# Hash attention and mixer: the products with v in four column tiles of 32, and one score block that begins with the bits

## The chip, the core and the metric

The kernel runs on one NeuronCore of a Trainium2 chip. The metric is the device time of one execution in microseconds; several executions are taken and the median is given. A profile of one execution comes with it: its span goes from the first to the last instruction of the program, and its engines are PE (TensorE, matrix products; PEld is its weight-load stream), DVE (VectorE), ACT (ScalarE), POOL (GpSimd) and SP (SyncE, which here only issues transfers).

## The reference

Attention over 4 batches, 8 heads, 768 tokens and 64 channels a head, in which a query sees only the keys of its own hash bucket, and then one mixer block whose input is the attention's output.

```python
q_bits = (einsum('bhsd,dk->bhsk', q, proj) > 0)      # 6 bits a token; k_bits likewise
mask   = q_bucket[..., :, None] == k_bucket[..., None, :]
scores = where(mask, q @ k.T / sqrt(64), -1e9)
attn   = softmax(scores)
x      = (attn @ v), heads side by side: (4, 768, 512)
h      = relu(x.T @ w_tok1) @ w_tok2                 # mixes tokens
u      = x + h.T
out    = u + relu(u @ w_ch1) @ w_ch2                 # mixes channels
```

All inputs but the four weight matrices are float32; the weights arrive as 64-bit floats and are turned into float32 on the chip.

## The kernel before

The program has three stages, one after the other: attention (from about 4 to 315 us of the span), the token mixing (to about 393 us) and the channel mixing. The change lies in attention alone.

Attention works on 16 pairs of heads (`pairs`, 4 batches by 4 pairs of heads). In a pair, q and k of both heads lie transposed in one tile, head i in partitions 64i to 64i+63. The 768 queries are cut into two halves of 384 (`Half`), the 768 keys into six blocks of 128 (`NR`). The order of the work is that of the program text: the stage runs under a manual schedule, and each engine works through its own instructions in the order in which the loop at L461 writes them.

For each half, `scores` (L328) makes six blocks. A block is a tile `sc` of 128 keys by two heads by 384 queries in PSUM, from a ring of three. Two products are added up in it: `product` at L334 with q and k (float32, 64 rows by 128 columns, one product a head, the two heads side by side in the array), and the same with `bits` (bf16). The rows of `bits` hold plus or minus one half for the query and a large multiple of it for the key, with one more row that cancels the sum when all bits agree, so that a key in another bucket gets a score so low that its exponential is zero. `exponential` (L342) takes the block to `e` on ACT, a tile in a ring of twelve. `add` and `add_last` sum the six tiles `e` of a half on DVE.

`hashes` (L292) makes the bits for the next pair: four products of 32 columns side by side (`hp`), a comparison on DVE (`g`), a scaling on ACT, and eight small transfers on SP into the rows of `bits` (L308). Block 0 of the next pair reads rows that the first four of these fill, the blocks from 3 on also those of the last four.

`weigh` (L380) multiplies with v: for each of six key blocks and each head one float32 product with the 64 columns of v as the weights, head 0 into partitions 0 to 63 of `acc` and head 1 into 64 to 127, so two column tiles of 64 side by side. ACT then takes `acc` to `num`. `Quotients.sums` (L407) sums the exponentials over keys with four products of 32 columns, `newton` and `divide` turn them into reciprocals and the result.

PE's order in pairs 1 to 14 is: six blocks of half 0, six blocks of half 1, `sums` of the pair before, `hashes` of the pair after, `weigh` of half 0, `weigh` of half 1. Pair 0 has no `sums` and makes its own hashes early; in its first half the first three blocks wait for those (`first`). Pair 15 makes no hashes and runs `sums`, `weigh`, `sums`, `weigh`. A float32 product appears in the trace as two matmul records and two weight loads, a bf16 product as one of each.

Of the kernel before, what the change touches and what calls it, by code (L numbers as in the profile page):

```python
# [48 lines left out]
def kernel(  # L49
# [13 lines left out]
    nc = tc.nc  # L63
    P = 128
    B, NP, _, _, S = qk.shape
    D = 64
# [4 lines left out]
    NR = S // P  # L71
# [186 lines left out]
    def attention(pool, psum, W1, W2, x0):  # L258
# [53 lines left out]
        def first_hashes(which, half):  # L312

            sl = slice(HALF * half, HALF * half + HALF)
            ps = psum.tile([P, 512], F32, name="hw", tag="sm" if which else "acc", bufs=1)[:, :HALF]
            nc.tensor.matmul(ps, projwide, loaded[0][0][:, which, sl], start=True, stop=True)  # L316
            to = bitrows[0][:, which, sl]
            nc.vector.tensor_scalar(to, ps, 0.0, 0.5, op0=ALU.is_gt, op1=ALU.subtract)  # L318
            if which:
                nc.vector.tensor_scalar(to, to, widescale, None, op0=ALU.mult)  # L320

        class Half:
# [5 lines left out]
            def scores(self):  # L328

                qkt, bits = loaded[self.n][0], bitrows[self.n % 2]  # L330
                qs = slice(HALF * self.half, HALF * self.half + HALF)
                first = self.n == self.half == 0

                def product(sc, t, c, start):  # L334
                    for i in range(2):
                        rows = slice(D * i, D * i + D)
                        nc.tensor.matmul(  # L337
                            sc[:, i, :HALF], t[rows, 1, P * c : P * c + P], t[rows, 0, qs],
                            start=start, stop=not start,
                        )  # L340

                def exponential(sc):  # L342
                    e = pool.tile([P, 2, HALF], F32, name="e", tag="e", bufs=12)
                    nc.scalar.activation(e, sc[:, :, :HALF], ACT.Exp, scale=SCALE)  # L344
                    self.es.append(e)

                waiting = []
                if first:
                    first_hashes(0, 0)
                    first_hashes(1, 0)  # L350
                for c in range(NR):
                    sc = psum.tile([P, 2, 512], F32, name="sc", tag="sc", bufs=3)
                    product(sc, qkt, c, True)
                    if first and c < GR:
                        waiting.append((c, sc))
                        if c == GR - 1:
                            for c, sc in waiting:
                                product(sc, bits, c, False)
                                exponential(sc)
                            first_hashes(1, 1)  # L360
                        continue
                    product(sc, bits, c, False)
                    exponential(sc)
                if first:
                    first_hashes(0, 1)
# [14 lines left out]
            def weigh(self):  # L380

                _, vn, _, vsum = loaded[self.n]
                if self.half:
                    acc = psum.tile([P, 2, 512], F32, name="acc", tag="sc", bufs=3)[:, 0, :HALF]
                else:
                    acc = psum.tile([P, 512], F32, name="acc", tag="acc", bufs=1)[:, :HALF]
                for c, e in enumerate(self.es):
                    for i in range(2):
                        nc.tensor.matmul(  # L389
                            acc[D * i : D * i + D], vn[:, i, c], e[:, i],  # L390
                            start=(c == 0), stop=(c == NR - 1),
                        )
                if self.half == 0:
                    nums[self.n] = pool.tile([P, 2, HALF], F32, name="num", tag="num", bufs=2)
                nc.scalar.activation(  # L395
                    nums[self.n][:, self.half], acc, ACT.Identity, scale=-1.0, bias=vsum,
                )
# [1057 lines left out]
```

## Time and profile before

| | |
|---|---|
| median of the runs | 802.52 us (3 runs, 801.86 to 803.08) |
| span of the profiled execution | 801.2 us |
| PE busy | 792.6 us, 99% of the span, 3885 matmuls |
| products with v (L389) | 768 matmul records of 488 ns, 768 weight loads of 137 ns |
| q-k products (L337) | 768 matmul records of 487 ns |
| bits' products (L337) | 384 matmul records of 323 ns |
| DVE busy, ACT busy | 657.8 us (82%), 441.6 us (55%) |
| exponentials (L344) | 192 of 811 ns |
| granted TensorE clock | 0.997 of full speed |

The profiled execution's own time was not recorded apart from its span; the median of the runs is 1.3 us above the span. A matmul's recorded length contains the time[...]the next one already runs, so the pace of PE is read from the starts of its records, not from their lengths. "64*128" beside a matmul is the rows by columns of the array that it uses. In brackets stands how long the engine was idle before and what released it.

### The profile page before, as it was taken

Reading aid. Unit: us, or ns where it says so; the run is one execution under the profiler, and the core shown is the slowest. Engines: PE = TensorE matmul, PEld = TensorE weight load, DVE = VectorE, ACT = ScalarE, POOL = GpSimd, SP = SyncE. Lnnn points to the kernel's source line nnn. Section 1 sums busy time; section 2 is a strip of 40 time slices with the busy share of each in tenths; the row PEclk is TensorE's granted clock in tenths of the full one; section 3 lists DMA queues with packets and bytes.
Section 4 is the critical chain, followed back from the end, with each engine's and each line's share of the span. In section 5 each row is a group of like instructions: output and inputs, shape, how many; then the busy total and the mean of one; then the engine's idle time right before and its main releaser. Section 6 shows DMA issues by size and latency. Waiting matters only on the chain.

```text
span 801.2 us, 10593 instructions
## 1 busy us (share of the span) xinstructions
PE 792.6 (99%) x3885; PEld 470.7 (59%) x3885; DVE 657.8 (82%) x881; ACT 441.6 (55%) x707; POOL 53.7 (7%) x77
## 2 busy tenths in 40 slices
PE   9999999999999999999999999999999999999996
PEld 5444444444444444455544458876667886666885
DVE  4889898989887677999677888988769897779986
ACT  5688888888888887333222221327783335775111
POOL 1000000000000000011121010011110012000010
PEclk9999999999999999999999999999999999999998
DMA  4435353537352424797636994599754578630455
GB/s 163 159 122 160 121 161 121 161 121 239 125 169 87 149 73 161 199 290 180 155 69 207 305 377 173 175 302 273 222 143 145 216 202 192 216 106 9 164 177 132
DMA packets 90972, 138.61 MB, mean 173 GB/s; under 512 B 29656, under 2 KB 63392, under 8 KB 88608
## 3 DMA queue, kind: packets, MB, share of 16 engines
q1 hardware_dynamic: 82480, 112.47, 42.4%
q0 software_dynamic: 7728, 24.64, 13.9%
q10 hardware_dynamic: 704, 0.74, 0.3%
q8 instruction: 33, 0.54, 0.3%
q14 instruction: 27, 0.22, 0.1%
HBM read 97.21 MB, written 33.16 MB: 163 GB/s over the span
## 4 chain that ended last, share of the span: by engine, by line
PE 99%; DVE 0%; ACT 0%; issue 0%
PE b L761 50%; PE sc L337 20%; PE acc L389 16%; PE t L634 5%; PE t L674 5%; PE sums L413 2%; PE hp L298 1%; PE hw L316 0%; PE idle L451 0%; DVE second L1184 0%; DVE bits L318 0%; ACT second L679 0%; DVE bits L320 0%; DVE ones L97 0%; PE b L1300 0%
## 5 line engine op out<-in xcount | busy, mean ns | idle before, releaser
L344 ACT ACTIVATE e<-sc 128x768 f32<-128x768 f32 x192 | 154.0, 811 | 12.4 <-PE sc L337 12.1
L337 PE MATMUL sc<-qk 64*128 64x384 f32 x768 | 156.7, 487 | 0.0
L761 PE MATMUL b<-R,second 128*128 128x256 f32 (+1 forms) x612 | 150.9, 404 | 0.0
L761 PEld LDWEIGHTS b<-R,second 128*128 128x128 f32 x612 | 116.3, 190 | 31.6 <-issue 17.2
L767 ACT COPY c<-b 128x512 f32<-128x512 f32 (+1 forms) x78 | 37.4, 488 | 169.1 <-PE b L761 158.5
L389 PE MATMUL acc<-e,vn 128*64 128x384 f32 x768 | 127.6, 488 | 0.0
L375 DVE TENSOR_TENSOR esd<-esd,e 128x768 f32<-128x768 f32 x96 | 92.0, 958 | 10.0
L389 PEld LDWEIGHTS acc<-e,vn 128*64 128x64 f32 x768 | 53.6, 137 | 73.1 <-issue 71.1
L337 PEld LDWEIGHTS sc<-qk 64*128 64x128 f32 x768 | 67.5, 187 | 49.1 <-issue 47.6
L761 PE MATMUL b<-XT,WC 128*128 128x256 f32 (+1 forms) x264 | 82.5, 457 | 0.0
L761 PEld LDWEIGHTS b<-XT,WC 128*128 128x128 f32 x264 | 50.2, 190 | 29.6 <-issue 24.9
L337 PE MATMUL sc<-bits 64*128 64x384 bf16 x384 | 62.9, 323 | 0.2 <-DVE bits L320 0.2
L371 DVE SCALAR_TENSOR_TENSOR esd<-e 128x768 f32<-128x768 f32 x32 | 30.6, 955 | 28.1 <-ACT e L344 28.1
L634 PE MATMUL t<-x,W 128*128 128x512 f32 x96 | 41.8, 593 | 0.0
L395 ACT ACTIVATE num<-acc,vsum 128x384 f32<-128x384 f32 x32 | 18.6, 582 | 31.7 <-PE acc L389 31.3
L694 POOL DMA_DIRECT2D XT<-second x8 | 9.9, 1232 | 391.6 <-DVE second L693 365.6
L434 ACT COPY rec<-rec 32x384 f32<-32x384 f32 x64 | 32.6, 510 | 5.0 <-DVE rec L428 4.2
L761 PE MATMUL b<-XT,SW 128*128 128x256 f32 (+1 forms) x120 | 34.6, 422 | 0.0
L337 PEld LDWEIGHTS <-bits 64*128 64x128 bf16 x384 | 19.3, 94 | 25.4 <-DVE bits L320 0.8
L761 PE MATMUL b<-TA,WC 128*128 128x512 f32 x72 | 33.8, 592 | 0.0
L761 PE MATMUL b<-TA,SW 128*128 128x512 f32 x72 | 32.9, 592 | 0.0
L378 DVE TENSOR_TENSOR esd<-esd,e 128x768 f32<-128x768 f32 x32 | 30.5, 954 | 1.9
(214 smaller groups left out, 1131.1 us busy)
## 6 DMA issues: line engine op xcount, KB each, us to landing
second<-left SPq DMA_DIRECT2D x18, 1344.0 KB
raw<-in_moe_w_ch SPq DMA_DIRECT2D x16, 768.0 KB
qk<-in_qk SPq DMA_DIRECT2D x15, 768.0 KB
seen<-in_qk POOLq DMA_DIRECT2D x21, 384.0 KB, 4.4
WC<-hidden_left SPq DMA_DIRECT2D x15, 448.0 KB
vn<-in_v SPq DMA_DIRECT2D x16, 384.0 KB
vt<-in_vT SPq DMA_DIRECT2D x16, 384.0 KB
x<-bounced SPq DMA_DIRECT2D x4, 1536.0 KB
```

The lines of the kernel that those rows point to most:

```text
L337: nc.tensor.matmul(sc[:, i, :HALF], t[rows, 1, P * c : P * c + P], t[rows, 0, qs], start=start, stop=not start,)
L344: nc.scalar.activation(e, sc[:, :, :HALF], ACT.Exp, scale=SCALE)
L371: nc.vector.scalar_tensor_tensor(self.d, es[0], NR * EPS, es[1], op0=ALU.add, op1=ALU.add,)
L375: nc.vector.tensor_tensor(self.d, self.d, e, op=ALU.add)
L378: nc.vector.tensor_tensor(self.d, self.d, self.es[-1], op=ALU.add)
L389: nc.tensor.matmul(acc[D * i : D * i + D], vn[:, i, c], e[:, i], start=(c == 0), stop=(c == NR - 1),)
L395: nc.scalar.activation(nums[self.n][:, self.half], acc, ACT.Identity, scale=-1.0, bias=vsum,)
L434: nc.scalar.copy(rec[other : other + 32, h], rec[at : at + 32, h])
L634: nc.tensor.matmul(ps, W1[:, r, P * j : P * j + P], x[:, r], start=(r == 0), stop=(r == NR - 1),)
L674: nc.tensor.matmul(ps[at], left, right, start=start, stop=True, skip_group_check=True,)
L761: nc.tensor.matmul(ps, left(k), right(k), start=start and k == ks[0], stop=stop and k == ks[-1], skip_group_check=True,)
L767: nc.scalar.copy(c, ps)
```

## The change

In `weigh` each product with the 64 columns of v is split into two of 32 columns. They read the same exponentials, take half of v's columns each as weights, and write 32 partitions of `acc` each, so that four column tiles of 32 stand side by side where two of 64 stood. In `scores`, block 0 of half 0 of every pair but the first makes the product of the bits first (it opens the sum in PSUM) and the product of q and k second (it closes it). The other eleven blocks of a pair keep their order.

```diff
@@ scores @@
                     sc = psum.tile([P, 2, 512], F32, name="sc", tag="sc", bufs=3)
+                    if c == self.half == 0 and not first:
+                        product(sc, bits, c, True)
+                        product(sc, qkt, c, False)
+                        exponential(sc)
+                        continue
                     product(sc, qkt, c, True)
@@ weigh @@
                     for i in range(2):
-                        nc.tensor.matmul(
-                            acc[D * i : D * i + D], vn[:, i, c], e[:, i],
-                            start=(c == 0), stop=(c == NR - 1),
-                        )
+                        for d in range(0, D, 32):
+                            nc.tensor.matmul(
+                                acc[D * i + d : D * i + d + 32], vn[:, i, c, d : d + 32], e[:, i],
+                                start=(c == 0), stop=(c == NR - 1),
+                            )
```

## Prediction

> **What bounds the kernel now.** I read the page first: busy shares, then the chain that ended last.
>
> ```profile
> PE 792.6 (99%) x3885; PEld 470.7 (59%) x3885; DVE 657.8 (82%) x881; ACT 441.6 (55%) x707; POOL 53.7 (7%) x77
> ...
> PE 99%; DVE 0%; ACT 0%; issue 0%
> ```
>
> The tensor engine's matrix stream is busy all the time and is the whole chain. So the change is worth what it takes out of, or puts into, PE's own sequence, unless it makes PE wait. The edit touches the attention stage only: 16 pairs of heads, from 4 to 315 us. Next I read one pair in the timeline of PE (start us, length us, what).
>
> ```profile
> 208.75 0.81 PE L337 MATMUL sc<-qk 64*128 64x384 f32 x4
> 209.39 0.33 PE L337 MATMUL sc<-bits 64*128 64x384 bf16 x2
> 209.65 0.85 PE L413 MATMUL sums<-esd,ones 128*32 128x384 f32 x8
> 210.32 0.83 PE L298 MATMUL hp<-qk,projs 128*32 128x384 f32 x8
> 211.08 7.96 PE L389 MATMUL acc<-e,vn 128*64 128x384 f32 x48
> 218.97 0.92 PE L337 MATMUL sc<-qk 64*128 64x384 f32 x4
> 219.72 0.33 PE L337 MATMUL sc<-bits 64*128 64x384 bf16 x2
> 219.88 0.81 PE L337 MATMUL sc<-qk 64*128 64x384 f32 x4
> ```
>
> Read the starts[...]. An f32 product is two records per tile. The single records, kept to the nanosecond, show one "pass" (the same record on all tiles side by side) starting every 0.322 us, for two tiles of 64 columns and equally for four of 32. The bf16 bits' pass takes 0.160 to 0.162. Against this grid the pair loses time in three places, and the single records give the same values in every pair:
> - the last score pass to sums: start to start 0.259 where 0.161 would do (0.098 lost), and the first pass of sums takes 0.347 (0.025 lost);
> - hashes (hp, tiles 128*32) to the products with v (acc, tiles 128*64): 0.436 for 0.322 (0.114 lost), and the first acc pass takes 0.373 (0.051 lost);
> - acc to the next pair's scores (64*128): 0.423 for 0.322 (0.101 lost), and the first qk pass takes 0.426 (0.104 lost), so that the first block lasts 0.911 where the others last 0.808.
> Between sums and hp, both 128*32, nothing is lost: 0.322. A pair lasts 19.21 us. The weight loads:
>
> ```profile
> 209.65 0.16 PEld L413 LDWEIGHTS sums<-esd,ones 128*32 128x32 f32 x8 [0.48 <-issue]
> 210.00 0.13 PEld L298 LDWEIGHTS hp<-qk,projs 128*32 128x32 f32 x4 [0.19 <-ACT e L344]
> 210.32 0.13 PEld L298 LDWEIGHTS hp<-qk,projs 128*32 128x32 f32 x4 [0.19 <-issue]
> 211.08 0.20 PEld L389 LDWEIGHTS acc<-e,vn 128*64 128x64 f32 x4 [0.62 <-issue]
> ```
>
> Four loads of 32 columns, 0.110 us each, end within 0.13 us: they run side by side, under the pass before (hp's first four start at 210.00, with the second sums pass). After a change of tile shape the first load starts only with its own pass, at 211.08, and is exposed.
>
> [...] about 0.1 us at each change of shape, none between sums and hp. [...] this trace has one such load exposed, in the first pair where PE waits for DVE:
>
> ```profile
> 9.36 0.92 PE L337 MATMUL sc<-qk 64*128 64x384 f32 x4
> 10.44 0.34 PE L337 MATMUL sc<-bits 64*128 64x384 bf16 x2 [0.16 <-DVE bits L320]
> 10.61 0.81 PE L337 MATMUL sc<-qk 64*128 64x384 f32 x4
> ```
>
> From the bits' pass to the next qk pass it is 0.173 by the single records, 0.012 above the usual 0.161. The f32 load of the qk pass, issued 3 ns after the bits' pass, was hidden under it.
>
> **The change part by part, working.**
> Part 1, acc in tiles of 32 columns. It adds 768 matmul records and 768 weight loads (24 passes a pair, four tiles for two). At the rate of sums and hp they are free: 0.322 a pass, loads side by side. What moves is the edges.
> - Pairs 1 to 14: hp to acc is no longer a change of shape. 0.114 + 0.051 = 0.165 saved; x14 = 2.31.
> - Pair 0 has no sums, and its acc follows scores: only the exposed load shrinks, 51 to 25 ns: 0.03.
> - Pair 15 runs sums, acc, sums, acc:
>
> ```profile
> 305.70 0.85 PE L413 MATMUL sums<-esd,ones 128*32 128x384 f32 x8
> 306.48 4.09 PE L389 MATMUL acc<-e,vn 128*64 128x384 f32 x24
> 310.50 0.85 PE L413 MATMUL sums<-esd,ones 128*32 128x384 f32 x8
> 311.28 4.09 PE L389 MATMUL acc<-e,vn 128*64 128x384 f32 x24
> 315.31 0.70 PE L634 MATMUL t<-x,W 128*128 128x512 f32 x1
> ```
>
>   Its edges: 0.165, then 0.422 for 0.322 plus 0.025 of load (0.125), then 0.165: 0.455.
> - Leaving acc still changes the shape, and now from four tiles, whose last starts 20 ns after the first instead of 7. The gap counted from the last tile is 0.416 both from hp (four) and from acc (two), so each of 16 exits costs 13 ns more: -0.21.
> Part 1: 2.31 + 0.03 + 0.455 - 0.21 = 2.59 us.
>
> Part 2, bits first in block 0 of half 0, pairs 1 to 15. Nothing is added, and no DMA, SP or POOL instruction moves; only PE's order does. The block becomes 0.161 + 0.012 + 2 x 0.322 = 0.817 for 0.911: 0.094 x 15 = 1.41 us.
>
> Covers. Part 2 brings the wait for the bits 0.75 us forward, to the head of a pair, where all of PE queues behind it, and ACT's exponentials and DVE's sums behind PE. Block 0 needs the first four of the eight bits transfers, issued on SP from 212.94 in this pair. By the DMA records they land at 214.5, 215.2, 215.9 and 216.8; the load would want them at about 218.8. In the tightest pair [...]the fourth lands by 198.4, wanted at 199.6. So 1.1 us of cover is the least; a later landing would cost its lateness once. The last four are needed at block 3, 2.4 us on. The PSUM ring: block 2 takes the buffer of the second acc, which ACT copies by 219.67; its load starts at 220.53. The reserve of 0.86 falls to 0.77. What could be late next is DVE or ACT: in this pair the windows show
>
> ```profile
> 209.65:228.86 19.21, 19.21 (x138) 9.21 (x136) 17.73 (x23) 16.13 (x25) 0.00 (x0) 1.00 0.51 141
> ```
>
> (length, then busy PE, PEld, DVE, ACT): DVE's 17.7 us and ACT's 16.1 still fit in 18.95.
>
> Sum: 2.59 + 1.41 = 4.00 us. After 315 us nothing changes, and what follows is 4 us earlier, because its loads and waits (the only long one, 0.55 us for ACT at 391.5) are tied to PE's progress. Profiled span 801.2 - 4.0 = 797.2. The median shown is 802.52, 1.3 us outside the span; I keep that: 798.5 us.
>
> What the trace does not show is four tiles kept up for 24 passes: sums and hp are four passes, 32 instructions in 1.3 us[...]. acc would need eight instructions every 0.322 us, 40 ns each. From below, the engine's own spacing in a group is 7 ns from tile to tile. From above, the 48 warm-up instructions of L451 run between 0.73 us, when PE's sequencer is released, and 3.41: at most 56 ns each. [...] One sign decides for me: in fifteen pairs the sequencer reaches the wait ahead of hp 0.11 us after the exponential that score block 11 waits for has ended, and 28 instructions lie between those two waits. That is a few ns each, if that exponential is what held it. I take no cost; bounds 0 and the rival below.
>
> **The rivals.**
> (a) Instructions do not come fast enough: slower. Place: acc only. [...] For it: a density never sustained in this trace. Against: the 0.11 us.
> (b) The bits' wait takes the place of the exposed load, or the qk load does not hide: part 2 gains nothing, 799.9. Against: the covers above and the pass at 10.44.
> (c) Part 1 does nothing, because acc's weights still cannot be loaded ahead or the four tiles read the same e twice and slip: only part 2 remains, 801.1. Against: hp follows sums with other weights and no loss. For: in sums and hp all four tiles hold the same weights, in acc four different ones.
> That the change doesn't do what it says is no case: both edits are plain instruction order and tile shape.
>
> **How the numbers follow.** Forecast as summed 0.74 (797.3 to 799.8), (b) 0.06, (c) 0.07, (a) 0.13. About 0.2%, 1.6 us, is what a measurement of this kernel can tell from no change. Faster takes the main case and (b): 0.80. Within 0.2% takes (c) and a mild (a): 0.10. Slower is the rest of (a): 0.10. The range ends where (b) and (c) do, 797.2 to 801.6; all but (a) lies inside. Its two bounds of unknown costs are 0 and (a), which is left out.
>
> **What would show it.** acc's rows: 1536 matmuls and 1536 loads of about 110 ns in 128*32; starts of passes 0.322 apart from sums through hp to acc; a first block that starts with the bits, its qk pass 0.17 later and the next block at 0.82; pairs of 18.95 us; PE still 99% of the chain. Wrong: pass starts that stretch over 0.322[...] of acc (a), a gap with a DMA as releaser ahead of the bits (b), 0.1 us still lost at acc's start (c), or DVE and ACT becoming releasers of PE.

## The result, and the profile after

The changed kernel takes 798.43 us (median of 6 runs, 797.46 to 800.01) beside 802.11 us for the kernel before (6 runs); the measured ratio is 0.9948, with a 95% interval of 0.9937 to 0.9960. The two medians by themselves differ by 3.7 us and give 0.9954, inside that interval. The forecast was 798.5.

The page of the changed kernel, its engine shares, the chain and the two rows of the products with v (out<-in, rows by columns of the array, shapes, count | busy us, mean ns | idle before):

```profile
PE 789.0 (99%) x4653; PEld 465.8 (59%) x4653; DVE 658.1 (83%) x881; ACT 441.9 (56%) x707; POOL 53.7 (7%) x77
...
PE 97%; DMA 1%; DVE 1%; issue 0%; ACT 0%; DVEq 0%; ACTq 0%
...
L395 PE MATMUL acc<-e,vn 128*32 128x384 f32 x1536 | 127.0, 486 | 0.0
...
L395 PEld LDWEIGHTS acc<-e,vn 128*32 128x32 f32 x1536 | 49.8, 110 | 74.0 <-issue 73.6
```

There are 768 more matmuls and as many more weight loads, and PE's busy time is 3.6 us less. PE is still 99% busy. The chain shows 1% of DMA because it now follows PE's one longer stop, at the end of the token mixing, back through a transfer (XT, 9.06 us from 378.11); that stop lasts 0.47 us (0.55 before) and is no part of the change.

The timeline of PE in the same pair as before:

```profile
207.67 0.85 PE L419 MATMUL sums<-esd,ones 128*32 128x384 f32 x8
208.34 0.83 PE L298 MATMUL hp<-qk,projs 128*32 128x384 f32 x8
208.99 7.92 PE L395 MATMUL acc<-e,vn 128*32 128x384 f32 x96
216.84 0.34 PE L337 MATMUL sc<-bits 64*128 64x384 bf16 x2
217.02 1.45 PE L337 MATMUL sc<-qk 64*128 64x384 f32 x8
218.31 0.33 PE L337 MATMUL sc<-bits 64*128 64x384 bf16 x2
```

Start to start, hp (the hash products of the next pair) now lasts 0.645 us (208.34 to 208.99) where it lasted 0.76: two passes and nothing else. The bits come first at 216.84, the qk pass follows 0.17 later; in the eight qk records that follow, block 1 begins behind block 0 without a gap. The weight loads at acc's start:

```profile
208.34 0.13 PEld L298 LDWEIGHTS hp<-qk,projs 128*32 128x32 f32 x4 [0.19 <-issue]
208.67 0.13 PEld L395 LDWEIGHTS acc<-e,vn 128*32 128x32 f32 x4 [0.19 <-issue]
208.99 0.13 PEld L395 LDWEIGHTS acc<-e,vn 128*32 128x32 f32 x4 [0.19 <-issue]
```

The first loads of acc start at 208.67, under the last pass of the hashes, 0.32 us ahead of their own pass. Before, they started with it.

By the single records every middle pair lasts 18.963 to 18.964 us, where each lasted 19.209 to 19.210. The time from the last of pair 0's own hash products (hw) to the first product of the token mixing was 302.561 us and is 298.573: -3.99. The spans of the two profiled executions differ by more, 5.5 us. The start is 0.34 us longer after the change: the first hash products begin at 3.75 us in both, but the clock record of the traces begins, with the full clock, at 5.11 us before and only at 5.78 us after. The passes of these products that start ahead of that take 0.80 and 0.60 us before and 0.80, 0.64 and 0.62 us after; without the change the next one, from 5.154, takes 0.324. The token stage is 0.08 us shorter, the channel stage equal to 0.001, and from the start of the last matmul to the end it is 1.80 us less (7.27 and 5.47). In the nine traces of this case the clock record begins anywhere from 3.9 to 6.6 us, and the spans of the six runs after go from 795.7 to 798.2, so I count the rest as scatter of the kernel's two ends.

### The profile page after: what moved, and what is told of

Read it like the earlier page. It is cut to its first block, busy times and chain, and to the rows that moved or that the text cites. A ratio compares the mean times of both kernels' runs of the same rounds, so it can differ in the third digit from the quotient of the medians.

```text
span 795.7 us, 12143 instructions
## 1 busy us (share of the span) xinstructions
PE 789.0 (99%) x4653; PEld 465.8 (59%) x4653; DVE 658.1 (83%) x881; ACT 441.9 (56%) x707; POOL 53.7 (7%) x77
## 4 chain that ended last, share of the span: by engine, by line
PE 97%; DMA 1%; DVE 1%; issue 0%; ACT 0%; DVEq 0%; ACTq 0%
PE b L767 50%; PE sc L337 20%; PE acc L395 16%; PE t L640 5%; PE t L680 3%; PE sums L419 2%; PE hp L298 1%; DMA XT<-second 1%; PE hw L316 1%; PE idle L457 0%; DVE second L1190 0%; DVE second L699 0%; DVE bits L318 0%; DVE second L697 0%; DVE second L695 0%
## 5 line engine op out<-in xcount | busy, mean ns | idle before, releaser
L337 PE MATMUL sc<-qk 64*128 64x384 f32 x768 | 152.6, 483 | 0.0
L395 PE MATMUL acc<-e,vn 128*32 128x384 f32 x1536 | 127.0, 486 | 0.0
L395 PEld LDWEIGHTS acc<-e,vn 128*32 128x32 f32 x1536 | 49.8, 110 | 74.0 <-issue 73.6
```

What stands on the lines that cost most here:

```text
L337: nc.tensor.matmul(sc[:, i, :HALF], t[rows, 1, P * c : P * c + P], t[rows, 0, qs], start=start, stop=not start,)
L395: nc.tensor.matmul(acc[D * i + d : D * i + d + 32], vn[:, i, c, d : d + 32], e[:, i], start=(c == 0), stop=(c == NR - 1),)
```

## The experiments

All ran beside the kernel before, on the same chip as it (median 802.95 us both times). Two undo one part each.

**The first part alone.**

```diff
-                    if c == self.half == 0 and not first:
-                        product(sc, bits, c, True)
-                        product(sc, qkt, c, False)
-                        exponential(sc)
-                        continue
```

> Part 1 alone (acc in four tiles of 32, every score block with q and k first). My theory: the gain sits on the edges of acc and the two parts add up. Hashes to acc 0.322 us start to start and the first acc pass 0.322, the exit of acc 13 ns longer, the first score block still 0.911 us; a middle pair 19.21 - 0.165 + 0.013 = 19.06 us; all pairs together -2.6 us, so about 799.5 beside 802.1, ratio 0.9968. Rival c (part 1 does nothing, all the gain is part 2's): a pair of 19.22 us and 802.3 us.

Measured: 800.01 us, ratio 0.9964 (0.9951 to 0.9977); each middle pair 19.058 to 19.059 us. PE's timeline:

```profile
209.58 0.83 PE L298 MATMUL hp<-qk,projs 128*32 128x384 f32 x8
210.22 7.92 PE L390 MATMUL acc<-e,vn 128*32 128x384 f32 x96
218.08 0.92 PE L337 MATMUL sc<-qk 64*128 64x384 f32 x4
218.83 0.33 PE L337 MATMUL sc<-bits 64*128 64x384 bf16 x2
218.99 0.81 PE L337 MATMUL sc<-qk 64*128 64x384 f32 x4
```

From the hashes to acc nothing is lost, and the first block still takes 0.91 us (218.08 to 218.99).

**The second part alone.** The loop over d in `weigh` is undone (two products of 64 columns).

> Part 2 alone (acc in two tiles of 64, block 0 of half 0 with the bits first). My theory: the first block lasts 0.817 us for 0.911, because the weight load that stands exposed after the change of tile shape is the bits' 12 ns instead of 104; a middle pair 19.21 - 0.094 = 19.12 us; 15 pairs -1.4 us, about 800.7 beside 802.1, ratio 0.9982. Rival b (the wait for the bits or the load of k under the short pass gives it back): a pair of 19.21 us or more, 802.1 us, with a transfer as the releaser ahead of the bits.

Measured: 801.55 us, ratio 0.9981 (0.9975 to 0.9987); each middle pair 19.114 to 19.115 us.

```profile
209.85 0.83 PE L298 MATMUL hp<-qk,projs 128*32 128x384 f32 x8
210.61 7.96 PE L394 MATMUL acc<-e,vn 128*64 128x384 f32 x48
218.50 0.34 PE L337 MATMUL sc<-bits 64*128 64x384 bf16 x2
218.67 1.45 PE L337 MATMUL sc<-qk 64*128 64x384 f32 x8
```

The 0.76 us of hp are back, the qk pass comes 0.17 after the bits. The savings of a pair, 0.151 and 0.095, add up to the 0.246 of the whole change.

**Is it the width or the neighbour?** Half 0 of acc in 64 columns, half 1 in 32:

```diff
+                width = 32 if self.half else 64
...
-                        for d in range(0, D, 32):
+                        for d in range(0, D, width):
```

> As the changed kernel, but acc of half 0 in two tiles of 64 and acc of half 1 in four of 32. My theory: what counts is whether neighbouring work has the same tile shape, not the width of the tiles. Then the edge from hashes to acc costs 0.165 us again and a new edge between the two halves of acc costs about 0.10 + 0.025: a middle pair 18.96 + 0.165 + 0.125 = 19.25 us, longer than before the change was made, and over 16 pairs about 4.6 us more than the changed kernel: 803. The other theory, that four tiles of 32 are quicker in themselves: half of part 1's gain stays, a pair of about 19.04 us, 799.7 us.

Measured: 803.53 us, ratio 1.0013 (1.0002 to 1.0024); middle pairs 19.251 to 19.253 us. The weight loads of acc around the seam:

```profile
215.28 0.14 PEld L396 LDWEIGHTS acc<-e,vn 128*64 128x64 f32 x2 [0.18 <-issue]
216.03 0.16 PEld L396 LDWEIGHTS acc<-e,vn 128*32 128x32 f32 x8 [0.60 <-ACT size L177]
216.38 0.13 PEld L396 LDWEIGHTS acc<-e,vn 128*32 128x32 f32 x4 [0.19 <-issue]
216.70 0.13 PEld L396 LDWEIGHTS acc<-e,vn 128*32 128x32 f32 x4 [0.19 <-issue]
```

Within either width loads and passes come every 0.322 us. At the seam the regular load at 215.61 is missing, the next ones start at 216.03, with their own pass, and both loads of a tile stand there (x8). The single records of all pairs give 0.422 to 0.423 us from the last 64-column pass to the first of 32, and 0.346 to 0.348 for that one: 0.100 and 0.025 lost. (The releaser named there, an ACT instruction, writes nothing that acc reads; the 0.100 is like the 0.098 to 0.114 lost at the other changes of shape.) So four tiles of 32 are no quicker than two of 64: 0.322 a pass for both. The gain is that their neighbours have that shape.

**Is it the order or the exposed load?** Block 0 of half 1 also takes the bits first (`if c == 0 and not first:`).

> As the changed kernel, but block 0 of half 1 also takes the bits first; ahead of it stands a score block of the same tile shape, so no weight load is exposed there. My theory: no change, a pair of 18.96 us, 798.4 us within 0.3. The other theory, that the order of the two products in a block is worth something in itself: another 0.094 us a pair, 1.4 us less, 797.0.

Measured: 797.40 us (4 runs), ratio 0.9933 (0.9918 to 0.9948), which overlaps the changed kernel's interval; middle pairs 18.963 to 18.964 us, as in the changed kernel. The median missed my 798.4 within 0.3 and lies nearer to the other theory's 797.0, but that theory needs pairs shorter by 0.094 us, and none is shorter; the two profiled executions differ by 0.2 us (797.25 and 797.46). So the order is worth nothing in itself. From the last hw product to the token mixing it is 298.477 us, 0.096 less than in the changed kernel, from one edge that I had overlooked: in pair 0 the hashes of pair 1 stand ahead of half 1's scores, so there, once, a load was exposed. This version is at least as good; the two can't be told apart by their medians.

**How near was a shortage of instructions?** The products with v cut along the queries, with the same arithmetic and more instructions (the diff is that of 192 queries; the second kernel has 96 in their place):

```diff
-                for c, e in enumerate(self.es):
+                for q in range(0, HALF, 192):
+                    for c, e in enumerate(self.es):
...
+                                    acc[D * i + d : D * i + d + 32, q : q + 192],
+                                    vn[:, i, c, d : d + 32], e[:, i, q : q + 192],
```

> As the changed kernel, but every product with v is cut into two of 192 queries, one group of 192 after the other, so that acc has 3072 matmuls and 3072 weight loads and needs eight instructions every 0.161 us, 20 ns each. It measures how near rival a was. My theory (an instruction costs PE's supply a few ns, and 7 ns is the spacing from tile to tile): passes 0.161 to 0.165 us apart to the end of acc, a pair of 18.96 to 19.1 us, 798.4 to 800.5 us. [...]

Measured: 799.54 us, ratio 0.9954 (0.9938 to 0.9971); pairs 19.023 to 19.024 us; passes 0.162 and 0.163 us apart to the end of acc. PE's timeline of acc in one pair:

```profile
209.30 7.98 PE L396 MATMUL acc<-e,vn 128*32 128x192 f32 x192
```

Twice the density costs 0.06 us a pair.

> The same with four groups of 96 queries: 6144 matmuls and as many loads in acc, eight instructions every 0.081 us, 10 ns each, and a load of 32 columns (110 ns in the rows) longer than the pass that it must hide under. My theory has no firm number here: if 3 to 4 ns an instruction were all, a pair of some 19.0 us and 799; if a pass can't be shorter than a load's 0.110 us, acc takes 96 x 0.110 = 10.6 us, a pair 21.8 us, 844; if the supply gives out at 20 ns, acc takes 15.1 us, a pair 26.3 us, 916.

Measured: 835.6 us in a single run. It is none of the three figures: passes are 0.082 and 0.083 us apart, shorter than the 0.110 us of a load's row, and go on so for some 41 passes (166 matmuls) before the first stop. PE's timeline of one pair:

```profile
188.95 3.64 PE L396 MATMUL acc<-e,vn 128*32 128x96 f32 x166
192.95 2.85 PE L396 MATMUL acc<-e,vn 128*32 128x96 f32 x128 [0.35 <-issue]
196.95 2.17 PE L396 MATMUL acc<-e,vn 128*32 128x96 f32 x90 [1.16 <-issue]
```

No wait releases PE after the stops ("issue"). Between the two stops lie exactly 128 matmuls and as many loads, here and in all eight pairs in which acc stops twice. The page's DMA part lists a queue for instructions (packets, MB, share of the DMA engines); in the changed kernel and in this one it reads

```profile
q8 instruction: 39, 0.64, 0.3%
```
```profile
q8 instruction: 75, 1.23, 0.6%
```

against 33 packets and 0.54 MB before. The change added 1536 instructions and 6 packets, 256 to 1; from the changed kernel to this one it is 9216 and 36, again 256 to 1. In the pair shown, packets land at 191.63 and 195.70, and PE goes on 1.3 us after each, at 192.95 and 196.95. The 256 instructions between the stops take 2.6 us at 10 ns each, and the packets there start 4.0 us apart. That PE waits for these packets is my estimate from these times and the count of 256; nothing was varied to show it. The stops are not the whole of the 835.6 us. Two of them are longer (3.6 us from start to start, from 27.65 us, and 3.3 us, from 338.40), and from 2.8 and 2.7 us after their beginning the clock record shows half the full clock, for 6.8 and 3.4 us.

**One edge more.** The hashes of pair 1 moved from between the halves of pair 0's scores to where other pairs have theirs (the call behind `scores` is dropped, `if 0 < n <` becomes `if n <`).

> As the changed kernel, but the hashes of pair 1 are made where those of the other pairs are, ahead of the products with v, and not between the two halves of pair 0's scores. My theory (every change of tile shape costs 0.10 us and the first load): in pair 0 an edge into the hashes' shape and one out of it go (0.094 + 0.025 + 0.114 + 0.104), and the edges that come in their place cost 0.094 + 0.104, with the way from scores to 32 columns paid as before: 0.14 us less in the attention stage, which the trace can show and the median cannot (798.3). Rival: the bits of pair 1 come 5 us later and PE waits for them at the head of pair 1: slower by the wait.

Measured: 800.78 us, ratio 0.9970 (0.9960 to 0.9980), slower than the changed kernel's 0.9948: 1.62 us more from the last hw product to the token mixing. My expectation missed and the rival held. PE's timeline at the head of pair 1 and ahead of it:

```profile
18.29 0.85 PE L298 MATMUL hp<-qk,projs 128*32 128x384 f32 x8
18.96 7.92 PE L395 MATMUL acc<-e,vn 128*32 128x384 f32 x96
27.90 0.32 PE L337 MATMUL sc<-bits 64*128 64x384 bf16 x1 [1.01 <-PE acc L395]
28.58 0.33 PE L337 MATMUL sc<-bits 64*128 64x384 bf16 x1 [0.36 <-DMA bits<-g]
```

The two heads' bits wait 1.01 and 0.36 us. acc had long been done when the first was released; the third transfer of the bits lands at 27.48 and the fourth at 28.22. They are late because the comparison on DVE starts at 23.00, 4.7 us after the start of the hashes (1.4 in later pairs), behind the sums of half 1 in DVE's queue. This is the kind of wait that part 2 would have met wherever the transfers landed after the head of the pair.

## Why the prediction was right

- *The path.* PE's own sequence set the end, and nothing else of size entered: the middle pairs agree within 0.001 us, and the change from the last hw product to the token mixing, -3.99, is the -4.00 of the sum.
- *Part 1.* Predicted 0.165 less at hp to acc and 0.013 more at the exit, 0.152 a pair; measured alone 0.151. Hashes to acc is 0.322 and the first acc pass 0.322. The gap from the last of four tiles to the scores is 0.416, as predicted, with part 1 alone, and 0.418 to 0.419 with the bits first. In pair 15 all three edges read 0.322.
- *Part 2.* Predicted 0.817 for the first block; the single records give 0.818 (0.173 for the bits, then 0.322 and 0.323). The one stalled bits pass of the trace before, 0.173, was the right row to price it from. A hidden bits pass is 0.162 to 0.163 in the records, not the 0.160 to 0.162 of the prediction, so the exposed load costs 0.011 rather than 0.012. Measured alone: 0.095 a pair for 0.094. That this fits to 0.001 is in part luck: two small terms that the sum did not have, the longer exit above (0.002 more) and the step from the last score pass to sums (0.255 to 0.256 for 0.259), nearly cancel.
- *The covers.* By the last of its 28 packets, the fourth transfer lands 2.0 to 2.2 us before the head of most pairs, and 1.5 us before it in the two tightest (7.6 before the head of pair 1). I had put the least at 1.1, because I took the end of a cluster of packets for the end of the fourth transfer. Pair 1 of the last experiment shows the case without cover.
- *Rival (a)* needed a rate of about 42 ns an instruction to cancel the gain (my estimate: 7.74 + 0.25 us over the 192 instructions of acc). With 192 queries 20 ns is sustained through whole acc stages, passes 0.162 and 0.163 us apart. With 96, at 10 ns, what came was no slower even rate but stops; where between 20 and 10 ns they begin, and what makes them, was not shown. There four matmuls start in every 0.0825 us, 21 ns each.
- *Rival (c)* fell with the first part alone: with four different weights loaded side by side (four loads in 0.13 us) and the same e read by two tiles, a pass of acc still takes 0.322 us.
- *The span* was forecast at 797.2 and came to 795.7; the 1.5 us are the ends of the execution named above, which no step of the sum spoke of.
- *The time*, 798.43, was within 0.1 of the forecast, and that closeness is partly luck. The 1.3 us added to the span set a median beside the span of one execution; every run that has both figures on record lies 1.7 to 1.9 us above its own span. By that the execution profiled before took about 803 us, at the upper end of its runs, and the one profiled after (797.46) is the fastest of its six. The medians differ by 3.7 us and not 4.0. What confirms the sum of 4.00 is the single records; the medians, with an interval of about 3 to 5 us, only agree with it.

## What to carry to other kernels

Where PE is busy without a break, lay its records on the grid of pass starts and look for passes that come late: here a change of tile shape cost 0.098 to 0.114 us (the trace before) and then the first weight load, which was 0.025, 0.051 and 0.104 us for float32 weights of 32, 64 and 128 columns and 0.011 for the bits' bf16 weights. Give neighbouring work the same shape, even if it means more instructions (here, at 20 ns each, they cost 0.06 us a pair), and let the load that can't be hidden be the cheapest one. Before moving an operand's use forward, look up when its transfer lands in every iteration, the first one too.

## What the runs showed of the hardware that I had not expected

With 96 queries PE kept up passes of 0.0825 us with four weight loads each, whose own rows read 0.110 us. At that density it stopped twice in one stage of 768 instructions, for 0.6 and 1.4 us from start to start, while the instruction packets started 4.0 us apart; that it waited for them is an estimate, as said above. In the same run, 2.8 and 2.7 us into the two stops of 3.6 and 3.3 us, the clock record fell to half the full clock. And doubling the number of passes at equal arithmetic (192 queries) cost about 2.5 ns for each added pass (0.06 us for 24).
